# Own-term products between the halves of the scores, y copied out by two engines, routing after the mask products

## The chip, the cores and the metric

The kernel runs on one core of one Trainium2 chip. The metric is the device time of one execution in microseconds; for a kernel, the median of several runs is given. Besides the timed runs there is one execution under the hardware profiler, and every row of a profile or trace in this document comes from such an execution. Engines are named as in the profile: PE is TensorE (matrix products), PEld its weight loads, DVE is VectorE, ACT is ScalarE, POOL is GpSimd, SP is SyncE.

## The reference

An attention block with a decaying state is followed by a layer of experts with sticky routing.

```python
for t in range(S):                                   # S = 768, per batch (4) and head (8), 48 features
    cur = einsum('bhd,bhe->bhde', u * k_t, v_t)      # the token's own term
    y[:, :, t] = einsum('bhd,bhde->bhe', r_t, state + cur)
    state = w * state + einsum('bhd,bhe->bhde', k_t, v_t)
x = y as (batch, token, 384)
logits = x @ w_gate; local = sigmoid(x @ w_local)
for b, s:                                            # in order of the tokens
    e = argmax(logits[b, s]) if s == 0 or local[b, s] < 0.5 else the expert of the token before
    out[b, s] = softmax(logits[b, s])[e] * (relu(x[b, s] @ w1[e]) @ w2[e])   # 8 experts, hidden size 1024
```

All of it is in 32-bit floating point.

## The kernel before, in words

**Stages.** Attention comes first (up to about 118 us of the profile's time), and the experts' products follow. The attention writes x to memory; gathers on POOL's queue then fetch the rows that each expert needs. Tokens are routed in two groups, batches 0 and 1 (group 0) and batches 2 and 3 (group 1). Group 0 is routed while the attention of batches 2 and 3 runs.

**Items.** An item is one batch and one pair of heads (`h` = 0, 1); there are 16 items, four to a batch. The 768 tokens of an item are six chunks of 128. A chunk `c` is written as `c = 2 * c2 + p`. The output of an item is the PSUM tile `y`, 128 partitions by two banks: `p` picks the half of the partitions, `h` the bank, `c2` a third of the bank. There is one `y` buffer (pool `py`, one buffer), so that an item's first write to `y` waits until the last item's `y` has been read.

**What is done for an item.** By function, with the line of the profile:

- `scale` (POOL, L216, L233, L220): keys with decay, `rw` (receptance with decay) and `pd` (receptance times key).
- `keys` (DVE, L240): `kw`, keys with the inverse decay.
- `scores` (PE L286, 24 products in two halves of three chunks, then DVE L288 for each half): the products of `rw` and `kw` go to one of two PSUM pairs of banks, and the mask product writes them to `am`. The mask product is either emitted at once (`self.scores(n, 0)()`) or kept for later (`keep = self.scores(n, 1)`, `keep()`).
- `own` (PE L267, four products, then DVE L271): the products of `pd` with `u` start the accumulation in `y`; DVE multiplies `y` in place by `v`.
- `added` (PE L251) and `states` (DVE L257, a scan): the states at the chunk borders. The products land in the bank `mp`, which routing also uses.
- `inside` (PE L295, twelve products): `am` with `v`, added to `y`.
- `before` (PE L308, ten products): states with `rw`, added to `y`. Then `y` is copied to `xT` (L312).
- `turn` (PE L321, ACT L323): six transposes of `xT`, copied to `x`; for every fourth item the batch's `x` goes to memory.
- `logits` (PE L334) and `token_logits` (PE L340), once a batch.

The trace shows each 32-bit product as two rows on TensorE, a transpose as one.

**Order.** Each engine executes its instructions in the order in which `run` emits them; no scheduler moves them. `run` loops over `n` = 0 to 16. For `n` from 3 to 15, iteration n emits in this order: `turn(n - 2)`, `keys(n)`, `added(n)`, `states(n)`, a piece of routing, `scale(n + 1)` for POOL, `inside(n - 1)`, `before(n - 1)`, first half of the scores of item n with its mask product, second half of the scores, another piece of routing, `own(n)`, and the second mask product. Where n is a multiple of four, the second mask product stands ahead of `own` and the batch's logits follow it. The loads of an item are issued on SP's queue three iterations ahead. Iterations 0 to 2 have branches of their own.

**Routing.** With `g` = 8 the pieces of group 0 are spread over iterations 9 to 15 (`experts_of`, `keys`, `runs`, `one_hot`, `counts`, `ranks`, `slots`, `columns`, `places`, `numbers`, `summed`, `copied`). `places` writes one of two halves of the one-hot tile `ohq` (DVE L781); `summed` (PE L788) needs both halves and stands between `inside` and `before` of iteration 15. Its result, by way of DVE L802 to L819, is the list `gid` for the first gathers (POOL L1035).

The copy of `y` before the change, which DVE shares only for the last item:

```python
for h in range(2) if n == B * HP - 1 else (slice(0, 2),):
    (nc.vector.tensor_copy if h == 1 else nc.scalar.copy)(
        self.xTs[t["b"]][:, 2 * t["hp"]:2 * t["hp"] + 2][:, h], t["y"][:, h, :C2 * P])
```

Of the kernel before, what the change touches and what calls it, by code (L numbers as in the profile page):

```python
# [21 lines left out]
B, H, S, DH = 4, 8, 768, 48  # L22
HP = H // 2
# [4 lines left out]
NCH = S // P  # L28
# [21 lines left out]
C2 = NCH // 2  # L50
# [10 lines left out]
class Attention:  # L61
# [198 lines left out]
    def own(self, n):  # L260

        nc, t = self.nc, self.items[n]
        t["y"] = y = self.py.tile([P, 2, 512], F32, name="y")
        for p in range(2):
            for h in range(2):
                q = slice(h * DP, h * DP + DH)
                nc.tensor.matmul(y[p * DP:(p + 1) * DP, h, :C2 * P].rearrange("p (c t) -> p c t", c=C2),  # L267
                                 lhsT=self.w_t[q, t["hp"], 1:2].to_broadcast([DH, DP]),
                                 rhs=t["pd"][q].rearrange("p (c k) t -> p k c t", k=2)[:, p],
                                 start=True, stop=True)  # L270
        nc.vector.tensor_mul(y[:, :, :C2 * P], y[:, :, :C2 * P], t["vT"].rearrange("p h c t -> p h (c t)"))  # L271
# [17 lines left out]

    def inside(self, n):  # L290
        nc, t = self.nc, self.items[n]
        for c in range(NCH):
            p, c2 = c % 2, c // 2
            for h in range(2):
                nc.tensor.matmul(t["y"][p * DP:(p + 1) * DP, h, c2 * P:(c2 + 1) * P],  # L295
                                 lhsT=t["v"][:, (2 * c + h) * DH:(2 * c + h) * DH + DP],
                                 rhs=t["am"][:, c // 3, h, c % 3], start=False, stop=False, skip_group_check=True)

    def before(self, n):
        nc, t = self.nc, self.items[n]  # L300
        if t["hp"] == 0:
            self.xTs[t["b"]] = self.late.tile([P, H, C2 * P], F32, name="xT")
            self.xs[t["b"]] = self.late.tile([P, NCH, D], F32, name="x", bufs=2)
        for c in range(1, NCH):
            p, c2 = c % 2, c // 2
            for h in range(2):
                q = slice(h * DP, h * DP + DH)
                nc.tensor.matmul(t["y"][p * DP:p * DP + DH, h, c2 * P:(c2 + 1) * P],  # L308
                                 lhsT=t["S"][q, :, c - 1], rhs=t["rw"][q, c],
                                 start=False, stop=True, skip_group_check=True)  # L310
        for h in range(2) if n == B * HP - 1 else (slice(0, 2),):
            (nc.vector.tensor_copy if h == 1 else nc.scalar.copy)(  # L312
                self.xTs[t["b"]][:, 2 * t["hp"]:2 * t["hp"] + 2][:, h], t["y"][:, h, :C2 * P])

# [28 lines left out]
    def run(self, router, fetch, heads):  # L343


        def pair(name):
            t = self.banks(name)
            return [t[:, 0], t[:, 1]]

        M = B * HP  # L350

        mp, mp_end = router.mp, 2 * P + 2 + (NCH - 1) * DH

        g = GROUPS[0][1] * HP
        for n in range(M + 1):
            if n + AHEAD - 1 < M:
                self.load(n + AHEAD - 1)
            elif n + 2 == M:
                fetch()
            if n == 0:  # L360
                self.scale(0)
                self.keys(0)
                self.tables()
                self.scores(0, 0)()
                self.scores(0, 1)()
                self.own(0)
                self.nc.scalar.copy(self.first, self.tab[:, 1, 0])
                self.turn_ends(slice(1, HP))
                self.warm(3)
                self.added(0)  # L370
                self.reciprocals(1)
                self.states(0)
                self.scale(1)
                continue
            if n < 3:

                self.keys(n)
                self.inside(n - 1)
                self.before(n - 1)
                if n == 2:  # L380
                    self.turn(0, pair("tp"))
                self.nc.scalar.copy(self.first, self.tab[:, n + 1, 0])
                self.scores(n, 0)()
                keep = self.scores(n, 1)
                self.own(n)
                if n == 1:
                    keep()
                self.added(n)
                self.states(n)
                if n == 2:  # L390
                    keep()
                else:
                    self.reciprocals(2)
                self.scale(n + 1)
                continue
            if n < M:
                self.turn(n - 2, pair("tp"))
                if n == 3:
                    self.added(3)
                    self.reciprocals(3)  # L400
                self.keys(n)
                if n > 3:
                    self.added(n)
            if n == g + 2:
                router.keys(0, mp)
            if n == g + 3:
                router.last(0, mp[:, mp_end:])
            if n == g + 4:
                router.counts(0, [mp, mp[:, E * NC // 2:]])
            if n < M:  # L410
                self.states(n)
            if n > HP and n % HP == 1:
                self.token_logits(n // HP - 1, pair("lq")[0])
            if n == 3:
                self.chooser()
            if n == g + 1:
                router.experts_of(0, (0,))
            if n == g + 2:
                router.runs(0)
            if n == g + 3:  # L420
                router.one_hot(0, (0,))
            if n == g + 4:
                router.ranks(0, (0,))
            if n == g + 5:
                router.slots(0)
                router.columns(0)
            if n == g + 6:
                router.numbers(0)
            if n == M:
                router.shares(0)  # L430
            if n + 1 < M:
                self.scale(n + 1)
            if 3 <= n < 6:
                router.constants(n - 3)
            if n == M:
                self.turn(M - 2, pair("tp"))
            self.inside(n - 1)
            if n == g + 7:

                router.summed(0, 0)  # L440
                router.copied(0)
            self.before(n - 1)
            if n == 6:
                router.cast()
            if n == M:
                break
            if n == g + 7:
                router.head(pair("tb")[0])
                heads()
            self.scores(n, 0)()  # L450
            keep = self.scores(n, 1)
            if n == g + 1:
                router.experts_of(0, (1,))
            if n == g + 3:
                router.one_hot(0, (1,))
            if n == g + 5:
                router.places(0, 0)
            if n == g + 6:
                router.places(0, 1)
            if n % HP == 0:  # L460

                keep()
                self.own(n)
                self.logits(n // HP - 1, pair("lp")[0])
                if n == g + 4:
                    router.ranks(0, (1,))
            else:
                self.own(n)
                keep()
            if n == g + 2:  # L470
                router.turn_runs(0, mp[:, mp_end:])
        self.inner.close()
# [81 lines left out]
class Router:  # L554
# [246 lines left out]
    def heads(self, table, out):  # L801
        self.nc.vector.tensor_reduce(out, table[:, :EARLY, :2], axis=AX.X, op=Alu.add)  # L802
# [160 lines left out]
class Experts:  # L963
# [49 lines left out]
    def fetch(self, i, engine):  # L1013
        u, wp = self.units[i], self.wps[i % 2]
        if i < EARLY:
            w1, w2 = self.w1[u["e"]], self.w2[u["e"]]
        else:
            e = self.nc.values_load(self.router.order[0:1, i - EARLY:i - EARLY + 1], engines=[ET.SP], min_val=0, max_val=E - 1,
                                    skip_runtime_bounds_check_because="the blocks' experts are a permutation")
            w1, w2 = [w[bass.ds(e, 1)].rearrange("o p x -> (o p) x") for w in (self.w1, self.w2)]  # L1020
        u["w1"] = wp.tile([P, FK, DK, P], F32, name="w1t", tag="w1t")
        engine.dma_start(out=u["w1"].rearrange("p m k f -> p (m k f)"), in_=w1)
        u["w2"] = wp.tile([P, FK, D], F32, name="w2t", tag="w2t")
        engine.dma_start(out=u["w2"].rearrange("p m f -> p (m f)"), in_=w2)
# [678 lines left out]
```

## Time and profile before

| What | Value |
|---|---|
| Median of 3 runs | 387.91 us (386.34 to 388.44) |
| The profiled execution | 388.46 us, of which the span is 386.7 us |
| Mean granted TensorE clock | 0.997 |
| PE busy | 373.9 us (97%) |
| DVE busy | 246.8 us (64%) |
| ACT busy | 107.8 us (28%) |
| POOL busy | 151.2 us (39%) |
| L312, copy of y to xT on ACT, whole | 15 rows, 0.80 us each |
| L288, mask product on DVE | 32 rows, 0.95 us each |
| L271, y times v on DVE | 16 rows, 0.96 us each |

A row of a timeline gives the start in microseconds from the start of the span, the time from the first start to the last end of the merged rows, the engine and line, the operation, output and inputs, the form, and how many instructions were merged; in brackets stands how long the engine was idle before the row and what ended that. Rows of TensorE overlap, because its products are pipelined and small products share the array; so the differences between starts tell more than the durations.

### The profile page before, as it was taken

How to read it: one execution, taken by the hardware profiler on the slowest of the kernel's cores; microseconds unless marked ns; L12 is line 12 of the kernel's file. 1: busy time of each engine (PE TensorE's matmuls, PEld its weight loads, DVE VectorE, ACT ScalarE, POOL GpSimd, SP SyncE). 2: the span in 40 equal slices, each digit the busy share in tenths (PEclk: the TensorE clock that was granted, in tenths of full speed). 3: DMA queues.
4: the chain of work that ended last, by engine and by line, in shares of the span. 5: the costliest groups of instructions: out<-in, count | busy, mean ns of one | idle time of the engine just before them, and what ended most of it. 6: DMA issues, size and time to landing. Idle time of an engine off the chain costs nothing. (4 is left out here: it accounts for less than half of the span.)

```text
span 386.7 us, 9723 instructions
## 1 busy us (share of the span) xinstructions
PE 373.9 (97%) x3858; PEld 330.7 (86%) x3858; DVE 246.8 (64%) x718; ACT 107.8 (28%) x293; POOL 151.2 (39%) x212
## 2 busy tenths in 40 slices
PE   7999998999999999999999999999999999999992
PEld 6776876877777999998999999999999999999971
DVE  6887577588854564587647757757757758556400
ACT  4122232222313111322323233234224234222220
POOL 7769999686422022611233222312403213012022
PEclk9999999999999999999999999999999999999998
DMA  7999998989412982650553145245146146054011
GB/s 258 412 409 412 407 400 271 323 300 335 153 32 96 381 331 73 240 194 23 184 171 116 42 170 210 69 171 204 55 185 225 37 165 225 24 196 183 2 37 37
DMA packets 17477, 74.97 MB, mean 194 GB/s; under 512 B 2729, under 2 KB 6586, under 8 KB 14864
## 3 DMA queue, kind: packets, MB, share of 16 engines
q1 hardware_dynamic: 10048, 56.89, 39.5%
q0 software_dynamic: 3424, 9.52, 7.4%
q10 hardware_dynamic: 3952, 7.87, 5.5%
q8 instruction: 32, 0.52, 0.5%
q14 instruction: 21, 0.17, 0.1%
HBM read 64.83 MB, written 9.51 MB: 192 GB/s over the span
## 5 line engine op out<-in xcount | busy, mean ns | idle before, releaser
L1261 POOL DMA_INDIRECT out_dram<-yo,sid x27 | 26.7, 987 | 102.2 <-ACT yo L1256 78.8
L1112 PE MATMUL h<-exT,w1t 128*128 128x168 f32 (+4 forms) x240 | 54.9, 327 | 0.0
L1116 DVE TENSOR_TENSOR hT<-h,hs 128x168 f32<-128x168 f32 (+3 forms) x60 | 21.0, 351 | 46.5 <-PE h L1112 30.5
L1035 POOL DMA_INDIRECT xg<-x_d,gid x29 | 31.1, 1072 | 38.2 <-DVE sm L870 17.4
L1112 PEld LDWEIGHTS h<-exT,w1t 128*128 128x128 f32 x240 | 41.7, 190 | 0.3 <-issue 0.3
L288 DVE TENSOR_TENSOR am<-pair,kept 128x768 f32<-128x768 f32 x32 | 30.1, 952 | 16.2 <-PE pair L286 15.8
L1062 PE MATMUL h<-exT,w1t 128*128 128x192 f32 (+1 forms) x192 | 38.2, 337 | 0.0
L1181 PE MATMUL y<-factors,sums 128*128 128x192 f32 x168 | 36.8, 326 | 0.0
L1112 PE MATMUL h<-xs,ws 128*128 128x168 f32 (+4 forms) x144 | 35.2, 326 | 0.0
L1062 PEld LDWEIGHTS h<-exT,w1t 128*128 128x128 f32 x192 | 32.3, 190 | 1.4 <-issue 0.2
L220 POOL TENSOR_TENSOR pd<-rk 128x384 f32<-128x384 f32 x32 | 31.8, 1012 | 3.0 <-DMA rk<-in_rk_dram 2.2
L295 PE MATMUL y<-am,kv 128*64 128x128 f32 x384 | 27.9, 278 | 1.6 <-issue 0.9
L1112 PEld LDWEIGHTS h<-xs,ws 128*128 128x128 f32 x144 | 25.5, 190 | 4.3 <-ACT hs L1119 1.2
L1181 PEld LDWEIGHTS y<-factors,sums 128*128 128x128 f32 x168 | 28.9, 190 | 0.0
L216 POOL TENSOR_TENSOR ke<-kv,endT 128x288 f32<-128x288 f32 x32 | 24.8, 794 | 3.9 <-DMA kv<-in_kv_dram 2.9
L295 PEld LDWEIGHTS y<-am,kv 128*64 128x64 f32 x384 | 24.0, 136 | 2.7 <-DVE y L271 1.2
L233 POOL TENSOR_TENSOR rw<-rk,tab 128x384 f32<-128x384 f32 x26 | 23.6, 925 | 6.8 <-PE y L308 6.8
L286 PE MATMUL pair<-rw,kw 48*64 48x128 f32 (+1 forms) x768 | 22.7, 249 | 1.2 <-ACT end L167 0.6
L312 ACT COPY xT<-y 128x768 f32<-128x768 f32 (+1 forms) x16 | 12.5, 780 | 40.5 <-PE y L308 40.5
L1181 PE MATMUL y<-w2t,hT 128*128 128x192 f32 x96 | 23.0, 328 | 0.0
L1049 DVE COPY exT<-tp 128x384 f32<-128x384 f32 (+6 forms) x29 | 14.0, 488 | 12.8 <-PE tp L1048 12.6
L286 PEld LDWEIGHTS pair<-rw,kw 48*64 48x64 f32 x768 | 19.6, 133 | 2.6 <-issue 0.9
(279 smaller groups left out, 739.1 us busy)
## 6 DMA issues: line engine op xcount, KB each, us to landing
w1t<-in_w_dram SPq DMA_DIRECT2D x9, 1536.0 KB, 6.8
w2t<-in_w_dram SPq DMA_DIRECT2D x9, 1536.0 KB, 7.5
rk<-in_rk_dram SPq DMA_DIRECT2D x15, 768.0 KB, 9.2
kv<-in_kv_dram SPq DMA_DIRECT2D x16, 584.0 KB, 9.0
vT<-in_vT_dram SPq DMA_DIRECT2D x16, 384.0 KB, 7.1
x_d<-x ACTq DMA_DIRECT2D x4, 1152.0 KB, 10.2
w1t<-in_w_dram ACTq DMA_DIRECT2D x1, 1536.0 KB, 10.3
w2t<-in_w_dram ACTq DMA_DIRECT2D x1, 1536.0 KB, 13.6
```

The costliest lines, as they stand in the source:

```text
L216: nc.gpsimd.tensor_mul(t["ke"][:, p::2], t["k"][:, p::2], spread(self.endT[:, p, hp], 1, C2))
L220: nc.gpsimd.tensor_mul(t["pd"][:, z], t["rT"][:, z], t["kT"][:, z])
L233: engine.tensor_mul(t["rw"][:, z], t["rT"][:, z], spread(pw, 1, z.stop - z.start))
L286: nc.tensor.matmul(sc[f * DP:(f + 1) * DP, h, i, x:], lhsT=t["kw"][q, c, o * DP:(o + 1) * DP], rhs=t["rw"][q, c, x:], start=True, stop=True)
L288: return lambda: nc.vector.tensor_mul(t["am"][:, g], sc, spread(self.kept[:, g:g + 3], 1, 2))
L295: nc.tensor.matmul(t["y"][p * DP:(p + 1) * DP, h, c2 * P:(c2 + 1) * P], lhsT=t["v"][:, (2 * c + h) * DH:(2 * c + h) * DH + DP], rhs=t["am" ...
L1035: self.nc.gpsimd.indirect_dma_start(out=xg[:n], out_offset=None, in_=self.x_d[:rows], in_offset=bass.IndirectOffsetOnAxis(ap=u["gid"][:n, ...
L1062: nc.tensor.matmul(h[:, :n], lhsT=u["w1"][:, m, kk, :], rhs=u["xT"][:, kk, :], start=(kk == 0), stop=(kk == DK - 1))
L1112: nc.tensor.matmul(out, lhsT=a, rhs=b, start=start and k == 0, stop=stop and k == len(terms) - 1, skip_group_check=True)
L1116: nc.vector.tensor_tensor(out, a, b, op=Alu.add)
L1181: return lambda: nc.tensor.matmul(bank[:, x * half:(x + 1) * half], lhsT=a, rhs=b, start=(j == 0 and x == 0), stop=(j == FK // 2 - 1), ski ...
L1261: self.nc.gpsimd.indirect_dma_start(out=out.rearrange("n (h d) -> (n h) d", h=2) if half else out, out_offset=bass.IndirectOffsetOnAxis(ap ...
```

## The change

Four things change, all in the attention stage.

- **Order of own and scores.** For n from 3 to 15, `own(n)` (its products and L271) is emitted between the two halves of the scores. The second half and its mask product follow at once. The kept mask product is gone, and so is the difference for every fourth item.
- **Copy of y.** For items 2 to 15, the copy from `y` to `xT` is two instructions: bank 0 on ACT, bank 1 on DVE. Before, this held for item 15 only.
- **Routing.** The second piece of routing of an iteration now follows the mask products instead of standing between them. `ranks` is placed there with the same iteration as before. The first half of `places` moves from iteration 13 to iteration 14, and the second half from iteration 14 to the first piece of iteration 15, behind `states`.
- **Order within own and inside.** The loop over `p` becomes the inner one, so that successive products alternate between the two halves of the output partitions; `inside` goes by `c2`, `h` and `p`.

```diff
@@ own
-        for p in range(2):
-            for h in range(2):
+        for h in range(2):
+            for p in range(2):
                 q = slice(h * DP, h * DP + DH)
@@ inside
-        for c in range(NCH):
-            p, c2 = c % 2, c // 2
-            for h in range(2):
+        for c2, h in [(c2, h) for c2 in range(C2) for h in range(2)]:
+            for p in range(2):
+                c = 2 * c2 + p
@@ before
-        for h in range(2) if n == B * HP - 1 else (slice(0, 2),):
+        for h in range(2) if n > 1 else (slice(0, 2),):
             (nc.vector.tensor_copy if h == 1 else nc.scalar.copy)(
@@ run
             if n == g + 6:
                 router.numbers(0)
+            if n == g + 7:
+                router.places(0, 1)
...
             self.scores(n, 0)()
-            keep = self.scores(n, 1)
+            self.own(n)
+            self.scores(n, 1)()
+            if n % HP == 0:
+                self.logits(n // HP - 1, pair("lp")[0])
             if n == g + 1:
                 router.experts_of(0, (1,))
             if n == g + 3:
                 router.one_hot(0, (1,))
-            if n == g + 5:
+            if n == g + 4:
+                router.ranks(0, (1,))
+            if n == g + 6:
                 router.places(0, 0)
-            if n == g + 6:
-                router.places(0, 1)
-            if n % HP == 0:
-
-                keep()
-                self.own(n)
-                self.logits(n // HP - 1, pair("lp")[0])
-                if n == g + 4:
-                    router.ranks(0, (1,))
-            else:
-                self.own(n)
-                keep()
             if n == g + 2:
```

## The prediction

> **What bounds the kernel now.** I read the page first: busy time, slices and chain. The profiled execution took 388.46 us for a span of 386.7 us, so 1.8 us lie around the span.
>
> ```profile
> PE 373.9 (97%) x3858; PEld 330.7 (86%) x3858; DVE 246.8 (64%) x718; ACT 107.8 (28%) x293; POOL 151.2 (39%) x212
> PE   7999998999999999999999999999999999999992
> ```
>
> TensorE is busy in every slice, and in the stretch table it is busy 245.00 of the 245 us from 120 to 365. The expert stage therefore has no slack: what the attention stage (0 to 116 us) gains or loses reaches the end one for one. So I looked at single items in the timeline. TensorE's timeline for iteration n=6, which finishes item 5 and starts item 6:
>
> ```profile
> 47.47 0.79 PE L308 MATMUL y<-rw,S 48*48 48x128 f32 x18
> 48.00 0.27 PE L286 MATMUL pair<-rw,kw 48*64 48x128 f32 x2
> 48.09 0.28 PE L308 MATMUL y<-rw,S 48*48 48x128 f32 x2
> 48.11 1.26 PE L286 MATMUL pair<-rw,kw 48*64 48x128 f32 x46
> 49.36 0.88 PE L267 MATMUL y<-pd,w_t 48*64 48x384 f32 x8
> 50.17 0.88 PE L321 MATMUL pair<-ident,xT 128*128 128x128 f32 x6
> 50.97 0.79 PE L251 MATMUL mp<-kv,ke 128*64 128x48 f32 x20
> 51.59 1.72 PE L295 MATMUL y<-am,kv 128*64 128x128 f32 x24
> ```
>
> I call B the start of an item's state products (L308), here 47.47. Differences of these starts give the phases: scores from B+0.53, own terms (L267) at B+1.89, transposes (L321) at B+2.70. Then 0.80 transposes, 0.62 added states and 1.65 products inside the chunks (L295); the next B comes 5.77 us later. Own at +1.89 and transposes at +2.70 recur in every iteration from 5 to 14 in which the state products are not late themselves (iterations 7 and 8 are). The last score starts at B+1.63, so even now 0.15 us or so of waiting stands before L267. VectorE and ScalarE in the same stretch:
>
> ```profile
> 48.87 0.96 DVE L288 TENSOR_TENSOR am<-pair,kept 128x768 f32<-128x768 f32 x1 [1.04 <-PE pair L286]
> 50.35 0.97 DVE L271 TENSOR_TENSOR y<-y,vT 128x768 f32<-128x768 f32 x1 [0.53 <-PE y L267]
> 51.23 0.95 DVE L288 TENSOR_TENSOR am<-pair,kept 128x768 f32<-128x768 f32 x1
> ...
> 48.41 0.80 ACT L312 COPY xT<-y 128x768 f32<-128x768 f32 x1 [2.41 <-PE y L308]
> ```
>
> ScalarE's copy out of y starts at B+0.95 and ends at B+1.75; L267, which overwrites the only y buffer, starts 0.14 later. So y's release already sets L267; the second half of the scores hides nearly all of it. The second mask product ends at 52.18, late for L295 from 51.59, which needs it halfway: 1.65 against 1.51 where nothing is late (iterations 11 to 13). That 0.14, more where routing stands between the products, is all that the rearrangement can win.
>
> The last item already has its copy cut between the two engines. The view of line L312 and the two timelines show how it runs:
>
> ```profile
> L312 DVE COPY xT<-y x1: 558/558/558, 116.6 to 116.6; 128x384 f32<-128x384 f32 x1
>   ACT xT L312: 2.4, 1
> 116.08 0.48 ACT L312 COPY xT<-y 128x384 f32<-128x384 f32 x1 [2.30 <-PE y L308]
> 116.60 0.56 DVE L312 COPY xT<-y 128x384 f32<-128x384 f32 x1 [2.37 <-ACT xT L312]
> ```
>
> VectorE's half waited for ScalarE's half and began 0.51 us after it. They run one after the other: 0.51 + 0.56 = 1.07 us until y is free, against 0.80 for the whole copy on ScalarE.
>
> **What the Trainium skill says.** PSUM — Partial Sum Buffer, "Specifications (TRN2)", has ScalarE and VectorE reading PSUM in parallel at full bandwidth as long as no bank collides. y's halves are different banks, so hardware would allow the parallel copy; the trace disagrees for this program, because of a wait between the instructions. In the changed kernel's compiled order each VectorE half carries that one wait, on ScalarE, and the first own-term product waits for VectorE. TensorE: Matmul & The Clock Gate, "Architectural detail", has ScalarE's and VectorE's queues strictly first-in first-out; the trace agrees, VectorE's order is the program's throughout. TensorEngine Tiling (Array Packing), "Key Properties", has tiles of one mode running independently and a change of mode draining the array: L267's four tiles start within 0.02 us, and the step from its last start to the transposes is 0.41 us, about 0.09 more than the 0.32 between its two passes.
>
> **The change part by part.**
>
> Copy in halves, items 2 to 14 (13 iterations, n=3 to 15; items 0 and 1 keep the whole copy, item 15 had the cut). y is free at B + 0.95 + 0.51 + 0.56 = B+2.02, and own starts 0.14 later: B+2.16, against 1.89.
>
> Own moved between the score halves. The first 24 scores end by about B+1.2, so TensorE stands for 0.95 us before L267, and 24 scores that covered the copy are queued behind L267's wait. From L267's start: 0.70 for its two passes (second start +0.37, +0.32), 0.50 to 0.55 for the scores (48 last start 1.1 us after the first), 0.2 for the last score and the change to the transposes' mode. That is 1.40 (estimate from these rows; bounds 1.3 and 1.5), so transposes at B+3.56 against 2.70: +0.86.
>
> Mask products. VectorE: its half copy ends at 2.02, first mask product about 1.95 to 2.9, L271 3.14 to 4.1 (0.99 after own, as now), second mask product 4.0 to 4.97. The inside products start at 3.56 + 0.80 + 0.62 = 4.98, so nothing is late: the 0.14 is won. VectorE gains 13 halves of 0.56 (7 us) but idles 1 us before its first mask product now, so this is hidden; ScalarE loses 0.32 an item, of no use because it idles 2 us before the copy. The transposes' bank is free at 2.9 (logits iterations: 4.97 against 4.99), just covered.
>
> Routing behind the mask products. Gains only what it delays now. Stalls of L295 over 1.51: 0.13 (n=3), 0.14 (5, 6, 7), 0.29 (9), and in iteration 13 0.36 plus 0.30 before it; 14 and 15 lose 0.36 too. Iterations 4, 8, 10, 11, 12 have none to win: L295 at iteration 8 stands for 1.1 us with no releaser, which I leave alone.
>
> The one-hot product moved past the scan. The routing sums (L788) follow item 14's inside products:
>
> ```profile
> 107.66 0.65 DVE L257 TENSOR_TENSOR_SCAN S<-step,mp 128x240 f32<-128x240 f32 x1
> 108.36 0.86 PE L788 MATMUL mp<-ohq,val 128*32 128x128 f32 x24 [0.34 <-DVE S L257]
> ```
>
> Both one-hot products (0.95 each) come an iteration later, so one stands before that scan and one behind it. Own scan end: B+6.38 becomes 7.28; the first half of L788 goes then, the second waits for the last one-hot, 8.1, and ends 8.56 instead of B+7.22. This iteration loses 1.34. The gathers issued from 111.22 get their list about 1 us later; their packets end at 115.1 and are used at 117.97, so 2.8 us cover it; without cover it would cost that 1 us.
>
> Halves alternated. L295's 24 starts take 1.31 where nothing is late, near 0.055 each, both array halves already overlapped: between 0.1 gained and 0.05 lost an item; I take 0. Own's reordering uses the same four tiles: 0. No DMA is moved; SP's and POOL's lists keep their contents, and POOL merely gets y's and pd's readers 0.27 later.
>
> Sum: n=3 +0.73; n=4 +0.51 (scores were late, own at 2.18 now); n=5, 6, 7 +0.72 each; n=8 +0.86; n=9 +0.57; n=10, 11, 12 +0.86 each; n=13 +0.19; n=14 +1.34; n=15 +0.36 (0.66 of its present waits goes, a first mask product later by the routing list gives 0.16 back). Total +9.3. On the profiled execution 388.46 + 9.3 = 397.8; on the median, 0.55 lower, 387.91 + 9.3 = 397.2.
>
> **The rivals.** *The halves run side by side*, as the change's words say. y free at B+1.51, own at 1.65, transposes at 3.05: +0.35 an item, less the same stalls, with iteration 14 as above: about +3.3, 391.2. Against it: the 2.37 us wait row.
>
> *The second half of the scores is the longer part*: if own to transposes takes 1.65, because scores and VectorE's second mask product run into the inside products, 13 x 0.25 is added: 400.4. For it: the second mask product has no margin (4.97 against 4.98, though needed only 0.45 later).
>
> *Not slower: TensorE carries the scores past the waiting own terms.* Two scores start 0.09 us before the last two L308 rows, so starts are not strictly in listing order. If all 24 slipped through, own at 2.16 and transposes at 2.97 would remain, and with 2.3 us of stalls removed the time would be 387 to 389. The point from which it decides: transposes no later than B+2.88 (2.70 plus the 0.18 that an iteration can win), i.e. y free by B+1.34, before either half alone could end (1.43). Against it: the pulled scores were not behind a waiting instruction, and now nothing slips past the wait before L267.
>
> **How the numbers follow.** Forecast 0.80 (395 to 400.5 by its own bounds: 13 x 0.1 either way, 1.3, alternation 13 x 0.1 down, the 1.1 us unexplained stand perhaps gone), side by side 0.08, longer scores 0.08, not slower 0.04. The range takes the forecast and part of the third: 393.5 to 401. 0.5% (1.9 us) is about what a measurement of this kernel can tell from no change. The not-slower case splits into faster 0.02, same 0.02; some of the side-by-side case falls near the bound, so same 0.03, slower 0.95.
>
> **What would show it.** Right: VectorE's L312 rows of 0.56 start 0.51 after ScalarE's; own at B+2.16 with an idle TensorE ahead of it released by VectorE's copy; periods near 6.5 us; L295 at 1.51; L788 split by a wait on the last one-hot. Wrong: own before B+1.9, or scores between the own terms' wait and their start. The prediction fails if VectorE's half starts with ScalarE's, or if TensorE's wait is worked off in the expert stage.

## The result, and the profile after

| | before | changed |
|---|---|---|
| Median | 387.88 us (6 runs, 386.34 to 388.44) | 395.81 us (6 runs, 395.65 to 396.53) |
| Ratio | | 1.0224 (95% interval 1.0207 to 1.0241) |
| Profiled execution, span | 388.46 us, 386.7 us | 396.53 us, 394.8 us |
| From item 2's state products to item 15's | 87.53 us | 95.71 us |

The changed kernel is slower by 7.9 us between the medians, and by 8.07 us between the profiled executions. The last row of the table is the difference of two starts of L308 in the trace. It grows by 8.18 us, so all of the loss lies in the attention stage, and the expert stage passes it on unchanged. Line numbers up to 390 are those of before; routing lines are five lower in the changed kernel (L776 is before's L781).

The page of the changed kernel: TensorE's busy time, and its slices.

```profile
PE 371.7 (94%) x3858; PEld 330.6 (84%) x3858; DVE 253.9 (64%) x731; ACT 103.4 (26%) x293; POOL 150.9 (38%) x212
PE   7998989888989999999999999999999999999992
```

The share falls from 97% to 94%, and only the slices of the attention stage changed. TensorE's timeline for iteration 6, the one that was shown of before:

```profile
49.34 0.81 PE L308 MATMUL y<-rw,S 48*48 48x128 f32 x17
...
50.08 0.72 PE L286 MATMUL pair<-rw,kw 48*64 48x128 f32 x23
51.52 0.88 PE L267 MATMUL y<-pd,w_t 48*64 48x384 f32 x8 [0.73 <-DVE xT L312]
52.19 0.76 PE L286 MATMUL pair<-rw,kw 48*64 48x64 f32 x24
52.88 0.88 PE L321 MATMUL pair<-ident,xT 128*128 128x128 f32 x6
53.69 0.79 PE L251 MATMUL mp<-kv,ke 128*64 128x48 f32 x20
54.31 1.50 PE L295 MATMUL y<-am,kv 128*64 128x128 f32 x24
```

TensorE stands idle ahead of the own terms (L267), and the bracket names VectorE's copy as what ended it; such an idle stretch of TensorE is called a stand below. Own terms start at B+2.18 here, and at B+2.16 in most iterations. The second half of the scores (the lower of the two L286 rows) now comes after the stand, and the transposes start at B+3.54. VectorE and ScalarE in the same stretch:

```profile
50.82 0.56 DVE L312 COPY xT<-y 128x384 f32<-128x384 f32 x1 [1.51 <-ACT xT L312]
51.30 0.95 DVE L288 TENSOR_TENSOR am<-pair,kept 128x768 f32<-128x768 f32 x1
52.46 0.97 DVE L271 TENSOR_TENSOR y<-y,vT 128x768 f32<-128x768 f32 x1 [0.21 <-PE y L267]
53.33 0.95 DVE L288 TENSOR_TENSOR am<-pair,kept 128x768 f32<-128x768 f32 x1
50.31 0.48 ACT L312 COPY xT<-y 128x384 f32<-128x384 f32 x1 [2.21 <-PE y L308]
```

VectorE's half starts 0.51 us after ScalarE's, that is 0.03 after its end. The view of waits gives the sums for TensorE between 20 and 125 us, in us, times and the longest:

```profile
PE y L267 <- DVE xT L312: 8.7, 11, 0.8
PE mp L672 <- DVE key L665: 1.0, 1, 1.0
PE mp L783 <- DVE S L257: 0.8, 1, 0.8
PE pair L286 <- issue: 0.8, 1, 0.8
```

Before, the largest sum in this view was 0.9 us, with no releaser named ("issue"):

```profile
PE y L295 <- issue: 0.9, 1, 0.9
```

Two of the changed kernel's rows are routing: L672 waits for the key, L783 for the scan.

### The profile page after: what moved, and what is told of

It reads as the page before. It is cut to its first block, busy times and chain, and to the rows that moved or that the text cites. A ratio compares the mean times of both kernels' runs of the same rounds, so it can differ in the third digit from the quotient of the medians.

```text
span 394.8 us, 9708 instructions
## 1 busy us (share of the span) xinstructions
PE 371.7 (94%) x3858; PEld 330.6 (84%) x3858; DVE 253.9 (64%) x731; ACT 103.4 (26%) x293; POOL 150.9 (38%) x212
## 5 line engine op out<-in xcount | busy, mean ns | idle before, releaser
L220 POOL TENSOR_TENSOR pd<-rk 128x384 f32<-128x384 f32 x32 | 31.5, 1006 | 4.4 <-PE y L267 2.9
L286 PEld LDWEIGHTS pair<-rw,kw 48*64 48x64 f32 x768 | 22.7, 133 | 6.6 <-issue 1.4
L286 PE MATMUL pair<-rw,kw 48*64 48x128 f32 (+1 forms) x768 | 25.9, 248 | 1.6 <-issue 0.8
L233 POOL TENSOR_TENSOR rw<-rk,tab 128x384 f32<-128x384 f32 x26 | 23.6, 929 | 8.5 <-PE y L308 8.3
L295 PE MATMUL y<-am,kv 128*64 128x128 f32 x384 | 25.0, 276 | 0.4 <-DVE y L271 0.4
L267 PE MATMUL y<-pd,w_t 48*64 48x384 f32 x128 | 14.0, 498 | 9.0 <-DVE xT L312 8.7
L295 PEld LDWEIGHTS y<-am,kv 128*64 128x64 f32 x384 | 21.1, 137 | 1.5 <-DVE y L271 0.7
```

The source lines that it names most:

```text
L220: nc.gpsimd.tensor_mul(t["pd"][:, z], t["rT"][:, z], t["kT"][:, z])
L233: engine.tensor_mul(t["rw"][:, z], t["rT"][:, z], spread(pw, 1, z.stop - z.start))
L286: nc.tensor.matmul(sc[f * DP:(f + 1) * DP, h, i, x:], lhsT=t["kw"][q, c, o * DP:(o + 1) * DP], rhs=t["rw"][q, c, x:], start=True, stop=True)
```

## The experiments

In all of them the steps are those of the prediction: B is the start of an item's state products, and a time of an iteration runs from one B to the next, so that it takes in the transposes, added states and inside products that the loop emits in its next pass. The first four share their runs of the kernel before (387.48 us, 19 runs); the second four do (389.79, 42 runs), and the last two (388.55, 19 runs). The time of the kernel before differs by up to 2.3 us between these comparisons, so I read each experiment from its own iterations as well as from its time. The experiments are called e1 to e10, in this order.

**The copy whole on ScalarE again.**

```diff
-        for h in range(2) if n > 1 else (slice(0, 2),):
+        for h in range(2) if n == B * HP - 1 else (slice(0, 2),):
```

> The changed kernel with y copied whole on ScalarE again for items 2 to 14 (item 15 stays cut); all else as changed. Theory (the two halves run one behind the other, so y is free 1.07 us after ScalarE starts against 0.80): own terms start at B+1.89 instead of B+2.16, transposes at B+3.25 instead of 3.52, 0.27 an iteration in 13 iterations, so about 3.5 us less than the changed kernel: 392.3 us. Rival (the cut helps, since each engine does half the work): 396 us or more, with own terms later than B+2.16.

Measured: 392.91 us, ratio to before 1.0148 (1.0116 to 1.0179); 2.9 us less than the changed kernel. The stand ahead of L267 in iteration 6 becomes shorter, and ScalarE releases it:

```profile
50.34 0.87 PE L267 MATMUL y<-pd,w_t 48*64 48x384 f32 x8 [0.54 <-ACT xT L312]
51.70 0.87 PE L321 MATMUL pair<-ident,xT 128*128 128x128 f32 x6
```

With B at 48.45, own terms start at B+1.89 and transposes at B+3.25: 0.27 less than with the cut copy, as expected, and an iteration takes 6.10 instead of 6.37. Cutting the copy costs; the rival falls.

**y as two tiles of one bank.** This changes the dependency; of the work only y times v changes, which becomes two products, and the copy is cut for items 0 and 1 too:

```diff
-        t["y"] = y = self.py.tile([P, 2, 512], F32, name="y")
+        t["y"] = y = [self.py.tile([P, 512], F32, name=f"y{h}") for h in range(2)]
...
-        nc.vector.tensor_mul(y[:, :, :C2 * P], y[:, :, :C2 * P], t["vT"].rearrange("p h c t -> p h (c t)"))
+        for h in range(2):
+            nc.vector.tensor_mul(y[h][:, :C2 * P], y[h][:, :C2 * P], t["vT"][:, h].rearrange("p c t -> p (c t)"))
...
-        for h in range(2) if n > 1 else (slice(0, 2),):
+        for h in range(2):
```

> The changed kernel with y as two tiles of one bank each in place of one tile of two banks; the cut copy then holds for all items and the product of y with v is two instructions. In the compiled order VectorE's half of the copy waits for TensorE and no longer for ScalarE. Theory (the order of the halves comes from y being one tile): both halves start at B+0.95, own terms at B+1.57 to 1.65, transposes near B+3.0, 0.5 us an iteration less in ten iterations and less in the three where TensorE waits for routing: about 6 us less than the changed kernel, 389.8 us. Rival (the two engines slow each other down when they read y at once, or VectorE's extra instruction costs as much): halves clearly longer than 0.48 and 0.56 us, or 394 us and above.

Measured: 390.48 us, ratio to before 1.0084 (1.0053 to 1.0115); 5.3 us less than the changed kernel. From the view of the copy's line (now L313; L309 is the state products) and the timelines of iteration 6:

```profile
L313 ACT COPY xT<-y x16: 478/479/480, 14.0 to 117.0; 128x384 f32<-128x384 f32 x16
L313 DVE COPY xT<-y x16: 489/556/558, 14.8 to 117.0; 128x384 f32<-128x384 f32 x16
48.75 0.48 ACT L313 COPY xT<-y 128x384 f32<-128x384 f32 x1 [2.17 <-PE y L309]
48.79 0.56 DVE L313 COPY xT<-y 128x384 f32<-128x384 f32 x1 [0.94 <-PE y L309]
49.37 0.89 PE L267 MATMUL y<-pd,w_t 48*64 48x384 f32 x8 [0.20 <-ACT xT L313]
```

Both halves start when the state products end, 0.04 us apart, and neither is longer than alone: the two engines did not slow each other here while they read two banks. So the order of the halves came from y being one tile. The parallel reading that the Trainium skill states (PSUM — Partial Sum Buffer, "Specifications (TRN2)") shows in this trace once the program allows it. Own terms start at B+1.55, and iterations 5, 6 and 7 take 5.78, just what they took before. What is left above before is then the later transposes in the iterations where nothing was late before (10 to 12, with routing 0.2 to 0.5 each), iteration 4 (0.7, see the stands below) and routing in 9 and 14 (1.0 and 0.9).

**Routing put back.**

```diff
             self.scores(n, 0)()
+            if n == g + 1:
+                router.experts_of(0, (1,))
+            if n == g + 3:
+                router.one_hot(0, (1,))
+            if n == g + 5:
+                router.places(0, 0)
+            if n == g + 6:
+                router.places(0, 1)
             self.own(n)
             self.scores(n, 1)()
...
-            if n == g + 1:
-                router.experts_of(0, (1,))
-            if n == g + 3:
-                router.one_hot(0, (1,))
...
-            if n == g + 6:
-                router.places(0, 0)
```

The later call `places(0, 1)` in iteration 15 is gone too.

> The changed kernel with the routing pieces back where they were: between the first mask product and y times v (experts_of, one_hot), and both halves of places in iterations 13 and 14. Theory (TensorE waits 1.0 us for the key, 0.2 us for the one-hot experts and 1.1 us more for the routing sums because these were moved back): the three waits go, iterations 9, 11 and 14 lose 1.1, 0.3 and 0.8 us, and a little comes back as late mask products in iterations 9, 11, 13: about 2 us less than the changed kernel, 394 us. Rival (routing behind the mask products is hidden or a gain, as the prediction had it for all but the sums): 395 us or more, iteration 9 not shorter.

Measured: 394.06 us (5 runs, 393.80 to 394.43), ratio to before 1.0176 (1.0149 to 1.0203); 1.75 us less than the changed kernel. Iteration 9 goes from 7.80 to 7.04, 11 from 7.42 to 7.12, 14 from 8.67 to 7.75; 13 rises from 6.37 to 6.55. TensorE's waits in the same window as above:

```profile
PE y L267 <- DVE xT L312: 8.9, 11, 0.8
...
PE mp L783 <- DVE S L257: 0.3, 1, 0.3
```

The row for the key is gone, and the one for the scan is down from 0.8 to 0.3. So moving the routing behind the mask products cost 1.75 us net. Of this 0.9 is iteration 14, which the prediction had; for the rest it had a small gain.

**Loops alternated, alone.** The first two hunks of the change, on the kernel before.

> The kernel before with only the loops within own and inside alternated. Theory (alternation alone shortens the inside products, first to last start 1.31 to 1.22 or 1.26 us): where nothing is late (iterations 4, 10, 11, 12) 0.05 to 0.09 less, where the second mask product is late no gain; 0.3 to 0.5 us in all, 387.5 us. Rival (the shorter inside products of the changed kernel come from the products and y being ready, not from the order of the loops): first to last start stays at 1.31 and the time at 387.9.

Measured: 387.67 us, ratio 0.9998 (0.9977 to 1.0019): no difference. In the trace the inside products of iterations 4, 8, 10, 11 and 12 take 1.26 us from first to last start, where before's (8 set aside, see below) take 1.31; in 5, 6, 7 and 13 they take what they took, because the second mask product is late there. So the alternation is worth 0.05 where nothing else holds the products, about 0.25 us in all, which the time can't show.

**The order alone.** On the kernel before, own terms between the halves and the second mask product at once; all else as before.

```diff
             self.scores(n, 0)()
-            keep = self.scores(n, 1)
...
+            self.own(n)
+            self.scores(n, 1)()
             if n % HP == 0:
-
-                keep()
-                self.own(n)
                 self.logits(n // HP - 1, pair("lp")[0])
...
-            else:
-                self.own(n)
-                keep()
```

> The kernel before with one part of the change: own terms between the two halves of the scores, second mask product at once; copy whole on ScalarE, routing pieces and loops where they were. Theory (24 scores that covered the copy now stand behind own terms' wait): own terms stay at B+1.89, transposes go from B+2.70 to B+3.25, the late second mask product goes; 0.4 an iteration where it was late, 0.55 where not, nothing in 13 to 15: 4 to 5 us more, 392 us. Rival (the order is what helps, and the cut copy alone is what costs): 387 us or less.

Measured: 392.35 us; ratio 1.0057 (1.0039 to 1.0074) against a before of 389.79 in this comparison. The steps are as expected: own terms at B+1.89, transposes at B+3.25, iterations 5 to 7 at 6.15 against 5.77, 10 to 12 longer by 0.55 to 0.63, 13 and 14 unchanged at 6.30 and 7.22. Its runs lie within 391.96 to 392.62, those of before within 387.73 to 391.79. The difference of the medians, 2.6 us, is below the 4 to 5 us expected; between the profiled executions (392.17 and 388.46) it is 3.7.

**The copy alone.** On the kernel before, the one line of the copy.

> The kernel before with one part of the change: the copy of y cut for items 2 to 14, y still one tile. Theory (halves one behind the other): own terms at B+2.16 behind all 48 scores, transposes at B+2.97 instead of 2.70; VectorE's products shift by as much, so the second mask product stays late by about 0.15: 0.27 in 13 iterations, 391 us. Rival (the second half of the scores hides the longer copy, as it hides the 0.80 now): 387.5 to 388.5 us, own terms below B+2.0.

Measured: 391.44 us; ratio 1.0050 (1.0036 to 1.0065) in the same comparison. TensorE's timeline in iteration 6, with B at 47.26:

```profile
47.89 1.27 PE L286 MATMUL pair<-rw,kw 48*64 48x128 f32 x46
49.42 0.88 PE L267 MATMUL y<-pd,w_t 48*64 48x384 f32 x8 [0.25 <-DVE xT L312]
50.22 0.87 PE L321 MATMUL pair<-ident,xT 128*128 128x128 f32 x6
```

All 48 scores stand ahead of own terms here and still don't cover the longer release: L267 waits to B+2.16, transposes start at B+2.96, an iteration takes 5.99 instead of 5.77. That is 0.22 rather than 0.27, since the second mask product is a little less late. The rival (hidden) falls. Here too the medians differ by less, 1.7 us, than the 3 us expected; the profiled executions (391.44 and 388.46) differ by 3.0.

**The routing alone.** On the kernel before, the pieces moved as in the change.

> The kernel before with one part of the change: the routing pieces behind the mask products, places an iteration later. Theory (TensorE waits for what is moved back): in iteration 9 the key is ready near B+5.75 and TensorE asks for it at B+4.2, in iteration 14 the routing sums wait for the scan and the last one-hot product, 1.3 us more; 0.7 comes back in iteration 13 and 0.3 in 9: 2 to 2.5 us more, 390 us. Rival (the routing only delays the mask products, so that moving it wins): 386 to 387 us.

Measured: 393.51 us, ratio 1.0092 (1.0063 to 1.0121), 3.7 us above before and more than I had expected. TensorE's waits (L677, L714 and L788 here are L672, L709 and L783 of the changed kernel):

```profile
PE mp L677 <- DVE key L670: 2.2, 1, 2.2
PE y L295 <- DVE y L271: 1.4, 1, 1.4
PE mp L788 <- DVE S L257: 1.2, 1, 1.2
PE mp L714 <- DVE oh L705: 0.8, 1, 0.8
```

Iteration 9 takes 8.44 (6.22 before) and 10 takes 7.30 (6.21). The stretch table shows another cause for the second; columns are busy time of PE, PEld, DVE, ACT, POOL, then the granted clock, the DMA share and GB/s:

```profile
70.00:75.00 5.00, 2.82 (x48) 2.19 (x46) 4.76 (x8) 0.70 (x2) 3.07 (x4) 0.96 0.90 349
75.00:80.00 5.00, 5.00 (x89) 4.09 (x89) 1.88 (x3) 0.99 (x3) 2.84 (x3) 0.70 0.82 284
```

After a stretch in which TensorE was busy for 2.82 of 5 us, the next had a granted clock of 0.70. In the changed kernel, whose wait for the key is 1.0 us, the same stretches show 4.19 and 3.98 us busy and a clock of 1.00 in both. Iterations 11 (7.19 against 6.35, a wait of 0.8 for the one-hot experts) and 15 (7.20 against 5.99, y times v late by 1.4) lose as well; the expectation had neither.

**A version meant to be faster than both.**

```diff
-        t["y"] = y = self.py.tile([P, 2, 512], F32, name="y")
+        t["y"] = y = [self.py.tile([P, 512], F32, name=f"y{h}") for h in range(2)]
...
-        for c in range(NCH):
-            p, c2 = c % 2, c // 2
-            for h in range(2):
+        for c2, h in [(c2, h) for h in range(2) for c2 in range(C2)]:
+            for p in range(2):
+                c = 2 * c2 + p
...
-            keep = self.scores(n, 1)
+            self.scores(n, 1)()
...
+            self.own(n)
             if n % HP == 0:
-
-                keep()
-                self.own(n)
                 self.logits(n // HP - 1, pair("lp")[0])
...
```

Not shown are the product of y with v, which is two instructions as above, the copy for all items, and `places` behind `own`.

> A version meant to be faster than both: the kernel before with y as two tiles of one bank, the copy cut for all items so that both halves run at once, both mask products ahead of y times v, loops alternated with the inside products going through one bank first, experts_of and one_hot between the mask products and y times v, places behind. Theory: y is free at B+1.51, so own terms follow the scores at B+1.75 without a wait, transposes at B+2.55, and no inside product is late: 5.4 to 5.5 us an iteration where it was 5.77, 3 to 4 us less, 384 us. Rival (VectorE's longer list, copy and cut product, or POOL with 5.2 us an item becomes the bound): 387 us or more.

Measured: 389.42 us, ratio 0.9985 (0.9965 to 1.0005): not told from before. Where nothing else holds it, an iteration does take 5.33 (5 and 13; before 5.77 and 6.30). But in 6, 7 and 8 own terms start at B+2.40, 2.52 and 2.78 instead of B+1.58. The view of waits has these rows (L309 is the state products here, L296 the inside products, L272 y times v):

```profile
PE y L296 <- DVE y L272: 1.9, 3, 1.2
PE y L309 <- issue: 1.8, 3, 0.8
```

The second row is iterations 6, 7 and 8: TensorE stood for 0.42, 0.54 and 0.80 us after the first three rows of the state products, with no releaser named, and own terms are late by that and 0.4 us more. POOL works without a gap from 39.9 to 65.7 us, but it was not late: its `pd` for items 6, 7 and 8 was done at 44.57, 49.90 and 55.25, at least 4.7 us before the own terms that read it (49.33, 55.51 and 61.95). So the time is in the rival's range, and VectorE's longer list does hold TensorE up in 9, 11, 14 and 15; but POOL is not what 6, 7 and 8 waited for. Iteration 9 (9.06 us) waited 0.7 us for the key and stood for 1.0 us with no releaser, and the granted clock fell to a mean of 0.71 in the 5 us after a stretch with 3.07 us of TensorE's work. In 14 the routing sums waited 1.2 us for the scan.

**The kernel before once more.**

> The kernel before, profiled once more. In the first profile TensorE stands 1.1 us inside the products of iteration 8 and 0.3 to 0.4 us in the state products of iterations 7 and 8 with no releaser named. Theory (these are stands of TensorE's own that come and go between executions): iteration 8 takes 8.0 to 8.3 us instead of 9.64, or a like stand shows elsewhere; every iteration without one repeats to 0.02 us. Rival (they belong to the program at that place): iteration 8 takes 9.6 us again.

The kernel is that of before, with no edit.

Measured: 388.73 us. Iteration 8 takes 8.63 instead of 9.64 (8.0 to 8.3 was expected), and iteration 9 takes 7.12 instead of 6.22, with a stand of 0.6 us that no release ended; 3, 5, 6, 10, 11, 12, 13 and 14 repeat to 0.01. So the long stand among the inside products has moved from iteration 8 to 9. Not all of the expectation holds: the smaller one in iteration 7 stays (6.05 after 6.04), and iterations 4 and 15 do not repeat (8.12 after 8.31, and 6.45 after 5.99, where the inside products wait 0.7 us for y times v instead of 0.2, for a reason that stays open). What the stands have in common is told at the end.

**The faster version with POOL relieved.** The version above, with one half of `pd` of items 5 to 9 on VectorE, issued first, and the two routing pieces between the mask products:

```diff
-            nc.gpsimd.tensor_mul(t["pd"][:, z], t["rT"][:, z], t["kT"][:, z])
+            engine = nc.vector if i and 4 < n < 10 else nc.gpsimd
+            engine.tensor_mul(t["pd"][:, z], t["rT"][:, z], t["kT"][:, z])
...
+        if 4 < n < 10:
+            pd(1)
...
```

> The version of the last batch (y apart, halves at once, mask products together) with two changes: one half of pd of items 5 to 9 on VectorE in place of POOL, issued first; and experts_of and one_hot between the two mask products. Theory (there own terms waited for POOL in iterations 6, 7, 8, 0.8 to 1.2 us each, and iteration 9 stood for the key): iterations 5, 6, 7 take 5.3 to 5.5 us, 8 about 7.8, 9 about 6.2 to 6.5; against the kernel before 2 to 3 us less, ratio 0.993 to 0.995. Rival (VectorE, which then carries the copy, the cut product and pd, is late instead, or routing needs the gaps): own terms or inside products late in 5 to 9, ratio 0.998 or above.

Measured: 389.43 us (14 runs, 386.39 to 393.66), ratio 0.9995 (0.9964 to 1.0027). The runs fall into groups: five lie between 386.39 and 386.74, about 2 us below before, three above 393; the profiled execution is one of the latter. The expectation rests on the reading that own terms waited for POOL in e8, which e8's trace does not bear out, and iterations 7, 8 and 9 miss it: with POOL relieved, 7 and 8 still take 6.38 and 8.79 (6.18 and 9.11 in e8), again with stands of 0.74 and 0.82 us inside the state products, and 9 takes 7.68. Iterations 5 and 6 take 5.33, but iteration 4 takes 13.85. Its VectorE and POOL timelines (L221, L237 and L317 are L220, L233 and L312 of before) and the stretch table:

```profile
33.09 4.34 DVE L221 TENSOR_TENSOR pd<-rk 128x384 f32<-128x384 f32 x1
37.35 0.54 DVE L317 COPY xT<-y 128x384 f32<-128x384 f32 x1
34.39 1.68 POOL L237 TENSOR_TENSOR rw<-rk,tab 128x384 f32<-128x384 f32 x2
36.03 0.99 POOL L221 TENSOR_TENSOR pd<-rk 128x384 f32<-128x384 f32 x1
35.00:38.00 3.00, 1.13 (x27) 0.46 (x19) 3.00 (x3) 0.00 (x0) 3.00 (x7) 0.85 1.00 406
38.00:41.00 3.00, 3.00 (x16) 0.84 (x20) 3.00 (x5) 0.00 (x0) 3.00 (x5) 0.50 1.03 414
```

The moved half of `pd` took 4.34 us on VectorE, from 33.09 to 37.43, while POOL multiplied without a gap until 37.02; the same operation took 0.74 at 45.17. The copy of y stood behind it, TensorE stood for 1.9 us, and then ran at a clock of 0.50. Of the five moved halves the other four took 0.63 to 0.74. None of the executions below 387 us was profiled, so it is not shown that the long `pd` is what sets the groups apart. No version here beats the kernel before beyond doubt.

## Why the prediction was right

The forecast was 397.2 us, in a range of 393.5 to 401.0; measured were 395.81. On the profiled executions it was +9.3, and +8.07 came.

**The release of y.** "The first 24 scores end by about B+1.2 ... own: B+2.16." Measured 2.16 in nine of the thirteen iterations, the halves 0.51 apart. The scores' part of the quotation is off: in these iterations TensorE is idle from B+1.35, and stands for 0.81 us instead of 0.95. That changed nothing, since the copy sets the start. That they run one behind the other was read from one item of the kernel before and from the compiled order; e1 and e2 show that it was the cause: the whole copy brings own terms to 1.89, the separate tiles to 1.55. Two readings of before were too wide: transposes do not start at B+2.70 in iterations 10 (2.86) and 12 (4.12, behind the logits), and the inside products that nothing delays, 1.51, are those of 10 to 12 and not of 11 to 13 (13 takes 1.87). The sum had used the right ones.

**From own terms to transposes.** "1.40 (estimate; bounds 1.3 and 1.5)": measured 1.36 (0.67 to the scores, 0.69 to the transposes). Transposes at B+3.52 instead of 3.56.

**The second mask product.** The forecast won back 0.14. VectorE's second mask product, forecast at B+4.0 to 4.97, runs from B+3.99 to 4.94 in iteration 6, and the inside products start at B+4.97, so nothing is late, as forecast. The inside products take 1.42 to the next B, against 1.65 before and 1.51 in the forecast. The other 0.09 is the alternation, which I had taken as 0 between 0.1 gained and 0.05 lost: 0.05 of it is measured by e4; the rest is that 1.51 came from iterations in which a routing product stands ahead of the inside products, where the changed kernel too takes 0.04 longer (1.26 against 1.22 from first to last start). Together, plain iterations grew by 0.60 to 0.62 where I had 0.72.

**Iteration by iteration** (us; 4 and 15, +0.70 and +0.18, were forecast at +0.51 and +0.36):

| Iteration | forecast | measured | why |
|---|---|---|---|
| 3, 5, 6 | +0.73, +0.72, +0.72 | +0.59, +0.60, +0.62 | the two sizes above |
| 7, 8 | +0.72, +0.86 | +0.36, -0.61 | stands of before that are smaller or not there |
| 9 | +0.57 | +1.58 | TensorE waits 1.0 for the key |
| 10, 12 | +0.86, +0.86 | +0.77, +0.80 | as 3, 5, 6 |
| 11 | +0.86 | +1.07 | 0.2 for the one-hot experts |
| 13 | +0.19 | +0.07 | as 3, 5, 6 |
| 14 | +1.34 | +1.45 | scan end forecast at B+7.28, sums start at 7.26, wait for the last one-hot product until 8.11 (forecast 8.1), end 8.5 |

**The step that failed** is "Routing behind the mask products. Gains only what it delays now." It asked what the routing delays, and not who waits for the routing. TensorE's transpose of the key (L672), which the loop emits in its next pass, stands ahead of that pass's inside products:

```profile
76.00 0.24 DVE L663 TENSOR_REDUCE k<-eq 128x12 f32<-128x96 f32 x1
76.28 0.17 DVE L664 TENSOR_TENSOR k<-t,k 128x12 f32<-128x12 f32 x1
76.48 0.76 DVE L665 SCALAR_TENSOR_TENSOR key<-lt,k 128x12 f32<-128x12 f32 x1
77.30 0.28 PE L672 MATMUL mp<-ident,key 128*12 128x128 f32 x1 [1.02 <-DVE key L665]
```

In the changed kernel the key's chain begins only at 76.00, 0.3 us before TensorE has finished the added states, and ends at 77.24. Before, it ran from 71.19 to 71.84, between the first mask product and y times v, and TensorE took it up at 73.14 without a wait:

```profile
71.67 0.17 DVE L670 SCALAR_TENSOR_TENSOR key<-lt,k 128x12 f32<-128x12 f32 x1
73.14 0.28 PE L677 MATMUL mp<-ident,key 128*12 128x128 f32 x1
```

e3 shows the same from the other side: put back, 1.75 us return. I had followed this question for the routing sums alone, and there the forecast held.

That the sum still came out too high has one more reason: about 1.8 us of iterations 7 and 8 in before's profile were stands with no releaser (6.04 and 9.64 there; 5.77 and 8.04 in e4, where only loops differ). The forecast left them in place in both kernels. The changed kernel's profile has one of 0.15 us or more: 0.8 us in iteration 4, inside the first half of the scores. Most of it falls where TensorE would wait for the copy anyway, but VectorE's first mask product starts 0.56 us later than in iteration 6, and iteration 4 takes 9.01 us where iteration 12 takes 8.73. That a kernel that waits at every item hides such stands would fit the narrower spread of the changed kernel, of e5 and of e6, but it was not tested.

That the total came so close is luck in part: of the 1.1 us between +9.3 and the 8.18 of the iterations, the forecast was 1.8 too high in 7 and 8 and 0.6 in 3, 5, 6, 10, 12 and 13, and 1.2 too low in 9 and 11. It is also by chance that the parts alone (2.6 for the order, 1.7 for the copy, 3.7 for the routing, 0.2 for the loops) add up to about the 7.9 us of the whole: within the change the copy costs 2.9 (e1) and the routing 1.75 (e3).

**The rivals.** Halves side by side: not so as the program stands; e2 makes it so and gives 390.48, where 391.2 was worked out for it. The longer second half: no, 1.36. TensorE carrying scores past the wait: none of the second half started before own terms in any trace.

## What to carry to other kernels

Two engines share a copy only if nothing in the program makes one wait for the other: here both read one tile, and the wait between them turned 0.80 us into 1.07. Look in the trace for a place where the cut already exists, and read when the second half starts. When a product that waits is moved ahead of other work, that work no longer covers its wait: here 24 scores came to stand behind it. And for a piece that is moved back, list its readers on the other engines as well as the work it stands in front of.

## What the runs showed of the hardware

A small operation of VectorE in SBUF became long when it started during a multiply of POOL. The key's operation on 128x12 elements, which has two inputs, took 0.17 us in the kernel before (both profiles), e4 and e5, where it starts in a gap of POOL, and 0.70 to 0.97 in the eight other profiles, where it starts 0.05 to 0.11 us into a multiply of POOL and ends within 0.03 us of its end. The reduction at the head of its chain (L663), which has one input, took 0.24 us in the changed kernel and before, though it ran within a multiply of POOL. POOL's timeline of the changed kernel:

```profile
74.37 1.96 POOL L220 TENSOR_TENSOR pd<-rk 128x384 f32<-128x384 f32 x2 [0.53 <-PE y L267]
76.43 1.54 POOL L216 TENSOR_TENSOR ke<-kv,endT 128x288 f32<-128x288 f32 x2
```

The first of the two `ke` multiplies runs from 76.43 to about 77.20 (half of 1.54), and the key from 76.48 to 77.24. The Trainium skill (SBUF — State Buffer, "Terms") has VectorE and GpSimd share a pair of ports under an exclusive lock, so that the loser blocks for the whole instruction; the durations agree, but no run here took POOL's work away to prove it. If it is so, 0.59 (0.76 less 0.17) of the 1.0 us wait for the key comes from it. The half of `pd` that took 4.34 us in e10 outlasted several multiplies of POOL, which a wait for one whole instruction does not explain.

The granted clock fell to 0.50 within the attention stage in three profiles: for 3.41 us in e7 (from 74.55) and e8 (from 74.49), and for 6.83 us in e10 (from 37.12), where the logits took 2.79 us instead of 1.50. TensorE was not idle all through the 3.41 us ahead of these falls: it was busy for 1.40, 2.00 and 1.85 us. The Trainium skill (TensorE: Matmul & The Clock Gate, "Part 1") gives half rate after an idle window; here a partly idle one was enough. Where the limit lies is not shown: two other stretches of 3.41 us in e7 (from 108.69 and 115.51), with 1.98 us busy, were followed by no fall. The changed kernel's waits of 0.7 to 1.0 us an item never brought it on: its clock stays at 1.00 from 5.5 us to the end of the attention stage, also after a stretch of 3.41 us with 2.37 us busy (from 114.73).

The stands with no releaser go together with the DMA packets of the kind "instruction". The page of the kernel before lists them:

```profile
q8 instruction: 32, 0.52, 0.5%
```

These are 32 packets of 16 KB for 7716 rows of TensorE and its weight loads, one for about 240 rows, which is near the 252 of an item. From iteration 3 on to the end of the attention stage, the twelve profiles hold 23 stands of 0.15 us or more with no releaser, and each of them ends 1.2 to 1.6 us after such a packet has landed, though the packets come about 6 us apart. In iteration 4 a stand shows in eleven of the twelve profiles, with 0.15 to 0.81 us; the others change their place. So TensorE seems to have waited for its own instructions there. No run changed the size or the order of the instruction stream alone, so this is not shown to be the cause.
